# Pooled attention and token-mixing MLP: scores of four heads in one group on the array's row halves

## The chip, the cores and the metric

The kernel runs on one core of a Trainium2 chip. The metric is device time in microseconds of one execution; the profile is of one execution of the same program. The engines run side by side, each with its own queue in order: TensorE (PE in the profile, with PEld for its weight loads), VectorE (DVE), ScalarE (ACT), GpSimd (POOL) and SyncE (SP), whose queue issues most of the transfers.

## The reference

Attention over pooled keys and values, for 8 batches of 8 heads, 576 tokens and 64 channels a head, and then a ResMLP layer over its output:

```python
k_p = k.reshape(B, H, Sp, pool, D).mean(axis=3)          # pool = 8, Sp = 72
v_p = v.reshape(B, H, Sp, pool, D).mean(axis=3)
attn = softmax(scale * np.matmul(q, k_p.transpose(0, 1, 3, 2)))
x = np.matmul(attn, v_p)                                  # heads side by side: (B, 576, 512)

a1 = alpha1 * x + beta1
u = x + lam * np.einsum('ts,bsd->btd', w_tok, a1)         # mixing over tokens
a2 = alpha2 * u + beta2
out = u + lam * (np.maximum(a2 @ w_ch1, 0.0) @ w_ch2)     # 512 -> 2048 -> 512
```

## The kernel before, in words

**Two pipelines side by side.** The MLP runs in nine blocks of 512 tokens. In a block, `mlp_A(n, j)` (16 steps, four products each, L555) makes 128 of the 2048 hidden channels and ScalarE applies bias and relu from PSUM (L560, tile Hj); `mlp_B(n, m, part)` (16 steps of four products, L573) then accumulates the output of 128 tokens at a time, and VectorE adds it to u (L578). While the MLP works on block n, the attention of batch n+1 is fed in between its steps. Batch 0 stands ahead of the blocks; the last two blocks have no attention beside them.

**The order is written by hand.** Every piece of work has a slot number, and `sorted` over these numbers gives the order in which instructions are put into the engines' queues. Step j of `mlp_A` has the slot j, and the steps of `mlp_B` have the slots 16 to 31. Each engine works its own queue in that order, so a slot says what stands ahead of what, not when it happens.

**The attention of a batch**, for batches 2 to 7:

- `att_F`, `att_Frem`: q transposed by DMA into qT (four heads a tile) and rem_qT (the last 64 tokens of all heads). In qT a head has its even and its odd tokens' channels on the two halves of the partitions; in rem_qT the halves are the even and the odd heads.
- `att_K(b, u)`: pooled and transposed keys of four heads, both halves of the partitions holding the same keys. VectorE copies each half into a tile kpT whose other half holds zeros (L416).
- `att_S(b, h)`: scores of one head. Against the zero-padded keys a product over all 128 partitions picks out one half: one product of 256 columns for each half (L450), one of 64 columns for the last 64 tokens (L453); ScalarE takes the exponential of each half into ET (L455).
- `att_V`: pooled values on VectorE.
- `att_AV(b, h)`: five small products (L470, L474) that also give the sum of the weights in a column of their own; VectorE takes the reciprocal (L476) and multiplies (L478).
- `att_X`: for two heads at a time x times lam and alpha1, on VectorE, into xs (L485 and the small half L489).
- `mix_T(b, c)`: the mixing over tokens, five products of 512 columns (L518) that read xs of all eight heads, for four chunks of 128 tokens; the last 64 tokens of two batches share a chunk. VectorE adds x (L522) and scales (L525), and `mix_uT` transposes the result for the MLP.

In the first batch of this loop (b=1) transposes of q are done on TensorE, the pooled keys are copied by ScalarE, and the constants of the mixing are still being set up.

**PSUM.** Two pools hold the eight banks: six tiles named gp, which serve scores, K, attention products, mixing and `mlp_A`, and two named ch, which `mlp_B` accumulates in. Tiles of a pool are handed round in order of request, and a request waits until the earlier holder of the same tile has been read.

The functions that the diff touches are these:

Of the kernel before, what the change touches and what calls it, by code (L numbers as in the profile page):

```python
# [7 lines left out]
FP = mybir.dt.float32  # L8
F16 = mybir.dt.float16
BF = mybir.dt.bfloat16  # L10
AF = mybir.ActivationFunctionType
# [3 lines left out]
P = 128  # L15
SPG = 72
DM = 512
# [6 lines left out]
def kernel(  # L24
# [18 lines left out]
    nc = tc.nc  # L43
    ctx.enter_context(tc.manual_schedule())
    B, H, S, D = q.shape

    const = ctx.enter_context(tc.tile_pool(name="const", bufs=1))
    work = ctx.enter_context(tc.tile_pool(name="work", bufs=1))
    psA = ctx.enter_context(tc.tile_pool(name="psA", bufs=6, space=bass.MemoryType.PSUM))
    psB = ctx.enter_context(tc.tile_pool(name="psB", bufs=2, space=bass.MemoryType.PSUM))  # L50

    def gp(name):
        return psA.tile([P, 512], FP, tag="gp", name=name)
# [11 lines left out]
    st1 = {}  # L65
# [164 lines left out]
    load_v16(0)  # L230
    load_wtok()

    vp1_pool, kpT_pool, ET_pool = [], [], []
    for i in range(4):
        t = const.tile([SPG, 2, 66], F16, tag=f"vp1_{i}", name=f"vp1_{i}")
        nc.vector.memset(t, 8.0)
# [1 line left out]
        if i < 2:  # L238
            t = const.tile([P, 2, 4, SPG], BF, tag=f"kpT_{i}", name=f"kpT_{i}")
            nc.vector.memset(t, 0.0)  # L240
            kpT_pool.append(t)
    for i in range(H):
        t = const.tile([SPG, S + 64], F16, tag=f"ET_{i}", name=f"ET_{i}")
        nc.vector.memset(t[:, S:], 1.0)
        ET_pool.append(t)
    xs_pool = [const.tile([P, 5, DM], BF, tag=f"xs_{i}", name=f"xs_{i}") for i in range(2)]
    nc.vector.memset(xs_pool[1][0:64, 4, :], 0.0)
# [143 lines left out]
    def att_K(b, u, copy):  # L391

        st = st1[b]
        ps_kp = gp("ps_kp")
        kp = ps_kp[:, 0:4 * SPG].rearrange("p (h g) -> p h g", g=SPG)
        n, nr = (1, 1) if b else (4, 2)
        if not b:
            nc.vector.tensor_copy(out=st["k"][u][:, :, 4], in_=st["k"][u][:, :, 0])
            if u == 0:
                cast_rem_k(nc.vector)  # L400
        for h in range(4):
            for c in range(n):
                nc.tensor.matmul(  # L403
                    out=kp[:, h, 0:64],
                    lhsT=st["k"][u][:, h, c:c + 2].rearrange("p a d -> p (a d)"),
                    rhs=pool_main, start=(c == 0), stop=(c == n - 1))
        for hh in range(2):
            for c in range(nr):
                nc.tensor.matmul(  # L409
                    out=kp[:, hh:4:2, 64:72],  # L410
                    lhsT=st["rem"][1][:, hh, c:c + 2].rearrange("p a d -> p (a d)"),
                    rhs=pool_rem.rearrange("p (g u r) -> p u r g", r=2, u=2)[:, u],
                    start=(c == 0), stop=(c == nr - 1))
        for a in range(2):
            rows = slice(64 * a, 64 * a + 64)
            (copy or (nc.scalar.copy, nc.vector.tensor_copy)[a])(  # L416
                out=kpT_pool[u][rows, a], in_=kp[rows])
# [16 lines left out]
    def att_V(b, hp):  # L434

        t = st1[b]["v"][hp // 2][:, 2 * (hp % 2):2 * (hp % 2) + 2]
        for n in (4, 2):
            nc.vector.tensor_tensor(out=t[:, :, 0:n], in0=t[:, :, 0:n], in1=t[:, :, n:2 * n],  # L438
                                    op=ALU.add)
        nc.vector.tensor_tensor(out=vp1_pool[hp][:, :, 0:64], in0=t[:, :, 0], in1=t[:, :, 1],  # L440
                                op=ALU.add)

    def att_S(b, h):
        st = st1[b]
        u, r, hh = h // 4, h // 2 % 2, h % 2
        ET = ET_pool[h]
        for half in range(2):
            n0, n = 256 * half, 256 + 64 * half
            ps_sc = gp("ps_sc")
            nc.tensor.matmul(out=ps_sc[0:SPG, 0:256], lhsT=kpT_pool[u][:, half, h % 4, :],  # L450
                             rhs=st["qT"][u][:, 2 * (h % 4):2 * (h % 4) + 2, :])
            if half:
                nc.tensor.matmul(out=ps_sc[0:SPG, 256:320], lhsT=kpT_pool[u][:, hh, h % 4, :],  # L453
                                 rhs=st["rem_qT"][:, :, h // 2::4].rearrange("p c i -> p i c"))
            nc.scalar.activation(out=ET[:, n0:n0 + n], in_=ps_sc[0:SPG, 0:n],  # L455
                                 func=AF.Exp, bias=0.0, scale=0.125)
        st["ET"][h] = ET

    def att_AV(b, h):
        st = st1[b]  # L460
        if "x" not in st:
            st["x"] = st1[b - 1]["x"] if b % 2 else work.tile([P, 6, DM], FP, tag="x_tm", bufs=1, name="x_tm")
        hp, hh = h // 2, h % 2
        ET, vp1, x = st["ET"][h], vp1_pool[hp], st["x"]
        ps_av = gp("ps_av")
        av = ps_av[:, 0:5 * 66].rearrange("p (c x) -> p c x", x=66)
        odd = b % 2
        for c in range(4):
            m0 = 256 * (c % 2) + 128 * (c // 2)
            nc.tensor.matmul(out=av[:, odd + c, :], lhsT=ET[:, m0:m0 + 128],  # L470
                             rhs=vp1[:, hh, :])

        r0 = 512 - 64 * odd
        nc.tensor.matmul(out=av[:, 4 - 4 * odd, :], lhsT=ET[:, r0:r0 + 128], rhs=vp1[:, hh, :])  # L474
        rec = work.tile([P, 5], FP, tag="rec", bufs=2, name="rec")
        nc.vector.reciprocal(out=rec, in_=av[:, :, 64:65])  # L476
        dd = D * h
        nc.vector.tensor_tensor(out=x[:, 1 - odd:6 - odd, dd:dd + D], in0=av[:, :, 0:64],  # L478
                                in1=rec.unsqueeze(2).to_broadcast((P, 5, D)), op=ALU.mult)

    def att_X(b, h0, h1, eng=nc.vector):

        x, xs = st1[b]["x"], xs_pool[b % 2]
        cols = slice(D * h0, D * h1)
        eng.tensor_tensor(  # L485
            out=xs[:, 0:4, cols], in0=x[:, 1:5, cols],
            in1=lamal_bc[:, cols].unsqueeze(1).to_broadcast((P, 4, D * (h1 - h0))), op=ALU.mult)
        p0 = 64 * (b % 2)
        eng.tensor_tensor(out=xs[p0:p0 + 64, 4, cols], in0=x[p0:p0 + 64, 5 - 5 * (b % 2), cols],  # L489
                          in1=lamal_bc[p0:p0 + 64, cols], op=ALU.mult)  # L490
# [177 lines left out]
    def attention(b):  # L668


        first = b == 1
        todo = []
        if first:
            for hp in range(4):
                todo.append((2.6 + 0.9 * hp, lambda hp=hp: att_F(b, hp)))
            todo.append((3.5, lambda: cast_rem(b, nc.gpsimd)))
            todo.append((3.65, lambda: load_w2(3)))
            todo.append((7.4, lambda: att_Frem(b, nc.scalar.copy)))
        if b == 2:
            todo.append((-2.0, lambda: cast_rem(b, nc.gpsimd)))  # L680
            todo.append((-1.1, lambda: att_F(b, 0)))
            todo.append((-1.1, lambda: att_F(b, 2)))
            todo.append((0.2, lambda: att_Frem(b)))
        if 1 < b < B - 1:
            at = 14.0 if b == 2 else 10.0
            todo.append((at, lambda: att_F(b + 1, 0)))
            todo.append((at + 0.1, lambda: att_F(b + 1, 2)))
            todo.append((27.4, lambda: cast_rem(b + 1, nc.gpsimd)))
            todo.append((27.5, lambda: att_Frem(b + 1)))
        for u in range(2):  # L690
            todo.append((3.6 + 0.1 * u if first else -0.9 + 1.2 * u,
                         lambda u=u: sum_k(b, u, nc.gpsimd)))
            todo.append((6.4 + 3.0 * u if first else 4.1 + 2.0 * u,
                         lambda u=u: att_K(b, u, nc.scalar.copy if first else nc.vector.tensor_copy)))
            if first:
                todo.append((11.0 + 1.2 * u, lambda u=u: first_V(b, u, nc.scalar.copy)))
        for h in range(8):
            at = 8.8 + 1.1 * h if first else 7.4 + 1.15 * h
            lag = 3.3 if first else 2.0
            todo.append((at, lambda h=h: att_S(b, h)))  # L700
            todo.append((at + lag, lambda h=h: att_AV(b, h)))
            if h % 2:
                eng = nc.gpsimd if first and h < 7 else nc.vector
                todo.append((at + lag + 0.1, lambda h=h, eng=eng: att_X(b, h - 1, h + 1, eng)))
            elif not first:
                todo.append((0.2 + 1.0 * h, lambda h=h: att_V(b, h // 2)))
        for c in range(5):
            at = 21.8 + 1.2 * c if first else 19.1 + 1.3 * c
            if c < 4 or b % 2:
                todo.append((at, lambda c=c: mix_T(b, c)))  # L710
                key = (b, c) if c < 4 else (b - 1, 4)
                if first and c in (2, 3):
                    at += 1.3 * c - 2.0
                elif first and c < 2:
                    at += 1.0
                todo.append((at + 1.8, lambda key=key: mix_uT(key)))
        return todo

    for n in range(NBLK):
        todo = []  # L720
# [14 lines left out]
        b = n + 1  # L735
# [46 lines left out]
```

The softmax here doesn't subtract the row's maximum and nothing guards it: scores larger than these inputs give would overflow.

## Time and profile before

| what | before |
|---|---|
| median of 3 runs | 361.68 us (361.34 to 361.83) |
| span of the profiled execution | 360.4 us |
| TensorE busy | 345.3 us, 96% |
| VectorE busy | 209.5 us, 58% |
| ScalarE busy | 154.1 us, 43% |
| GpSimd busy | 86.6 us, 24% |
| mlp_A and mlp_B products, L555 and L573 | 138.1 and 133.7 us busy, 592 and 576 products |
| score products, L450 and L453 | 25.4 and 15.6 us busy, 128 and 64 products |
| exponentials, L455 | 44.8 us busy, 128 of them |

A product's busy time holds the passage through the array, which overlaps with the next product, so the spacing of starts says more of the cost than the busy time. A line of the timeline has the start, the length from the first start to the last end, the engine, the source line, the operation with what it writes and reads, shape and count, and in brackets the idle time ahead of it with what ended it. A line of a group ends with the busy time, the mean of one instruction in ns, and the engine's idle time before the group.

### The profile page before, as it was taken

What the parts mean: (1) busy time and instruction counts of PE and PEld (TensorE: products, weight loads), DVE (VectorE), ACT (ScalarE), POOL (GpSimd) and SP (SyncE); (2) the same over time, 40 slices, a digit from 0 to 9 for tenths busy, and PEclk for the clock granted to TensorE, in tenths of its full rate; (3) what the DMA queues carried; (4) which work ended last, traced back from release to release, by engine and by line L of the source; (5) the groups of instructions that cost most, each with busy time, mean ns of one, the idle gap of its engine ahead of it and who ended that gap; (6) DMA issues with size and microseconds to landing.
All of it is one profiled execution on the core that took longest, in us unless ns stands there. A gap on an engine that the chain in (4) does not pass through costs nothing.

```text
span 360.4 us, 5916 instructions
## 1 busy us (share of the span) xinstructions
PE 345.3 (96%) x2229; PEld 186.7 (52%) x2229; DVE 209.5 (58%) x452; ACT 154.1 (43%) x319; POOL 86.6 (24%) x99
## 2 busy tenths in 40 slices
PE   4988999899999999999999999999999999999994
PEld 1566765445644564456445644564456445545541
DVE  6484347688773778576748787677567870011011
ACT  2572995027900890069006900592059204704700
POOL 8469407261117000620052006200510000000000
PEclk9999999999999999999999999999999999999999
DMA  8999920977949872987199729872910132011012
GB/s 122 200 215 261 216 43 3 185 189 203 162 118 225 155 125 64 244 159 126 53 206 190 130 62 215 175 131 60 224 58 0 40 78 75 0 58 60 1 58 58
DMA packets 65886, 44.58 MB, mean 124 GB/s; under 512 B 32377, under 2 KB 57021, under 8 KB 65858
## 3 DMA queue, kind: packets, MB, share of 16 engines
q1 hardware_dynamic: 50480, 33.30, 38.6%
q0 software_dynamic: 15072, 10.76, 20.9%
q8 instruction: 17, 0.28, 0.3%
q10 hardware_dynamic: 306, 0.14, 0.2%
q14 instruction: 11, 0.09, 0.1%
HBM read 38.30 MB, written 9.44 MB: 132 GB/s over the span
## 4 chain that ended last, share of the span: by engine, by line
PE 89%; DVE 4%; ACT 3%; DMA 2%; SPq 1%; issue 1%; ACTq 0%; DVEq 0%
PE ps_ch L573 33%; PE ps_h L555 32%; PE ps_tok L518 11%; PE ps_sc L450 4%; PE ps_av L470 2%; DVE x_tm L478 2%; PE ps_sc L453 1%; ACT Hj L560 1%; DMA vecs<-in_moe_alpha_dram 1%; PE ps_bc L278 1%; PE ps_kp L403 1%; DMA rem_qT<-rem_q 1%; SPq L363 1%; DVE w L339 1%; PE ps_q L368 1%
## 5 line engine op out<-in xcount | busy, mean ns | idle before, releaser
L560 ACT ACTIVATE Hj<-ps_h,bias_cols 128x512 bf16<-128x512 f32 x144 | 98.8, 690 | 150.8 <-PE ps_h L555 149.9
L555 PE MATMUL ps_h<-u_fm,w 128*128 128x512 bf16 (+1 forms) x592 | 138.1, 374 | 1.4 <-ACT u_fm L541 1.1
L573 PE MATMUL ps_ch<-w,Hj 128*128 128x512 bf16 x576 | 133.7, 379 | 0.0
L573 PEld LDWEIGHTS <-Hj 128*128 128x128 bf16 x576 | 54.7, 98 | 62.7 <-issue 1.6
L555 PEld LDWEIGHTS <-w 128*128 128x128 bf16 x592 | 63.3, 114 | 45.7 <-issue 2.6
L578 DVE TENSOR_TENSOR u_sb<-u_sb,ps_ch 128x512 f32<-128x512 f32 x36 | 24.5, 688 | 75.1 <-PE ps_ch L573 74.7
L518 PE MATMUL ps_tok<-xs,wtT 128*128 128x512 bf16 (+3 forms) x200 | 44.5, 380 | 1.8 <-DVE xs L485 1.8
L455 ACT ACTIVATE ET<-ps_sc 72x256 f16<-72x256 f32 (+1 forms) x128 | 44.8, 405 | 2.6 <-PE ps_sc L450 2.5
L522 DVE TENSOR_TENSOR u_sb<-x_tm,ps_tok 128x512 f32<-128x512 f32 (+1 forms) x40 | 27.5, 687 | 19.5 <-PE ps_tok L518 19.4
L478 DVE TENSOR_TENSOR x_tm<-ps_av,rec 128x320 f32<-128x320 f32 x64 | 31.5, 492 | 2.5
L147 POOL CAST rem_q<-rem_raw 128x256 bf16<-128x256 f32 x7 | 2.9, 421 | 123.0 <-DMA rem_raw<-in_q_dram 123.0
L518 PEld LDWEIGHTS <-wtT 128*128 128x128 bf16 (+3 forms) x200 | 17.3, 100 | 23.6 <-issue 1.8
L438 DVE TENSOR_TENSOR v_u<-v_u 72x512 f32<-72x512 f32 (+1 forms) x48 | 27.5, 573 | 1.2
L525 DVE TENSOR_TENSOR u_bf<-u_sb,al_bc 128x512 bf16<-128x512 f32 x34 | 26.3, 775 | 1.2
L450 PE MATMUL ps_sc<-qT,kpT 128*72 128x256 bf16 x128 | 25.4, 278 | 0.1
L476 DVE RECIPROCAL rec<-ps_av 128x5 f32<-128x5 f32 x64 | 12.3, 192 | 21.1 <-PE ps_av L474 20.2
L470 PEld LDWEIGHTS <-ET 72*128 72x128 f16 x256 | 16.0, 97 | 11.9 <-issue 0.5
L162 POOL TENSOR_TENSOR k_raw<-k_raw 128x512 f32<-128x512 f32 x14 | 18.2, 1303 | 14.1 <-DMA k_raw<-in_k_dram 13.6
L164 POOL TENSOR_TENSOR k_bf<-k_raw 128x512 bf16<-128x512 f32 x14 | 19.0, 1354 | 1.1
L485 DVE TENSOR_TENSOR xs<-x_tm,lamal_bc 128x512 bf16<-128x512 f32 x26 | 18.3, 704 | 0.9
L470 PE MATMUL ps_av<-vp,ET 72*128 72x66 f16 x256 | 18.0, 193 | 0.3 <-ACT wtT L299 0.3
L416 DVE CAST kpT<-ps_kp 64x288 bf16<-64x288 f32 x26 | 11.8, 455 | 10.5 <-PE ps_kp L409 5.2
(111 smaller groups left out, 217.5 us busy)
## 6 DMA issues: line engine op xcount, KB each, us to landing
out_dram<-u_sb SPq DMA_DIRECT2D x32, 256.0 KB
k_raw<-in_k_dram SPq DMA_DIRECT2D x14, 512.0 KB
v_u<-in_v_dram SPq DMA_DIRECT2D x12, 512.0 KB
q_bf<-in_q_dram POOLq DMA_DIRECT2D x16, 256.0 KB, 7.0
w<-in_moe_w_ch_dram POOLq DMA_DIRECT2D x8, 512.0 KB, 11.3
v<-in_v_dram POOLq DMA_DIRECT2D x4, 256.0 KB, 7.5
out_dram<-u_sb SPq DMA_DIRECT2D x8, 128.0 KB
rem_raw<-in_q_dram SPq DMA_DIRECT2D x15, 64.0 KB
```

The costliest lines, as they stand in the source:

```text
L438: nc.vector.tensor_tensor(out=t[:, :, 0:n], in0=t[:, :, 0:n], in1=t[:, :, n:2 * n], op=ALU.add)
L450: nc.tensor.matmul(out=ps_sc[0:SPG, 0:256], lhsT=kpT_pool[u][:, half, h % 4, :], rhs=st["qT"][u][:, 2 * (h % 4):2 * (h % 4) + 2, :])
L455: nc.scalar.activation(out=ET[:, n0:n0 + n], in_=ps_sc[0:SPG, 0:n], func=AF.Exp, bias=0.0, scale=0.125)
L470: nc.tensor.matmul(out=av[:, odd + c, :], lhsT=ET[:, m0:m0 + 128], rhs=vp1[:, hh, :])
L478: nc.vector.tensor_tensor(out=x[:, 1 - odd:6 - odd, dd:dd + D], in0=av[:, :, 0:64], in1=rec.unsqueeze(2).to_broadcast((P, 5, D)), op=ALU.mult)
L518: nc.tensor.matmul(out=ps_tok[p0:p1], lhsT=wtT[0:kk, at, P * c:P * c + p1 - p0], rhs=xs_pool[i][0:kk, sc, :], start=(sc == 0), stop=(sc == 4))
L522: nc.vector.tensor_tensor(out=s["u"][p0:p1, :], in0=x[p0:p1, 1 + c if c < 4 else 5 - 5 * i, :], in1=ps_tok[p0:p1, 0:DM], op=ALU.add)
L525: eng.tensor_tensor(out=s["u_bf"], in0=s["u"], in1=al2_bc, op=ALU.mult)
L555: nc.tensor.matmul(out=ps_h[:, t0:t1], lhsT=w1_of(cc, j), rhs=u_fm[n][:, cc, t0:t1], start=(cc == 0), stop=(cc == 3))
L560: nc.scalar.activation(out=t, in_=ps_h, func=AF.Relu, bias=bias_cols[:, j:j + 1], scale=1.0)
L573: nc.tensor.matmul(out=ps, lhsT=Hj[n, j][:, 128 * m:128 * m + 128], rhs=w2[j // 4][:, j % 4, :], start=(j == 0), stop=(j == NJ - 1))
L578: nc.vector.tensor_tensor(out=u, in0=u, in1=ps, op=ALU.add)
```

## The change

For batches 1 to 7 the scores of four heads become one group, `att_S4(b, u)`. The keys are no longer padded with zeros: `att_K` copies them once into kp, and each product contracts over 64 partitions, on one half of the array's rows, so that the products of the even and of the odd tokens can work side by side. The two halves write to tiles of their own: four tiles of the pool gp and both of the pool ch, which `mlp_B` doesn't use in these slots. The exponentials then take 512 columns at a time (two heads of one half), and two more take the last 64 tokens of two heads each. The order of heads within a group becomes 2, 3, 0, 1; the attention products are given slots after the exponentials, and the mixing starts half a slot later. Batch 0 keeps its scores as they were.

```diff
+            kp_pool.append(const.tile([P, 4, SPG], BF, tag=f"kp_{i}", name=f"kp_{i}"))
-    for i in range(H):
-        t = const.tile([SPG, S + 64], F16, tag=f"ET_{i}", name=f"ET_{i}")
-        nc.vector.memset(t[:, S:], 1.0)
+    for i in range(2):
+        t = const.tile([SPG, 4, S + 64], F16, tag=f"ET_{i}", name=f"ET_{i}")
+        nc.vector.memset(t[:, :, S:], 1.0)
...
+        if b:
+            copy(out=kp_pool[u], in_=kp)
+            return
...
+    def att_S4(b, u):
+
+        st = st1[b]
+        qT, kp, rest = st["qT"][u], kp_pool[u], st["rem_qT"]
+        lo = [psB.tile([P, DM], FP, tag="ch", bufs=2, name="ps_s") for _ in range(2)]
+        hi = [gp("ps_s") for _ in range(2)]
+        r = [gp("ps_r")[0:SPG, 0:128].rearrange("p (h i) -> p h i", i=64) for _ in range(2)]
+
+        for i in range(4):
+            a = i % 2
+            nc.tensor.matmul(
+                out=r[a][:, i // 2], lhsT=kp[64 * a:64 * a + 64, i, :],
+                rhs=rest[64 * a:64 * a + 64, :, 2 * u + i // 2::4].rearrange("p c i -> p i c"))
+
+        for i in (2, 3, 0, 1):
+            for a in range(2):
+                rows = slice(64 * a, 64 * a + 64)
+                nc.tensor.matmul(
+                    out=(hi if i > 1 else lo)[a][0:SPG, 256 * (i % 2):256 * (i % 2) + 256],
+                    lhsT=kp[rows, i, :], rhs=qT[rows, 2 * i:2 * i + 2, :])
...
+        def exp(k):
+            if k < 2:
+                o, i = ET[:, k::2, 512:S], r[k]
+            else:
+                a, pair = k % 2, (hi, lo)[k // 2 - 1]
+                h = 2 if k < 4 else 0
+                o = ET[:, h:h + 2, 256 * a:256 * a + 256]
+                i = pair[a][0:SPG, :].rearrange("p (h i) -> p h i", i=256)
+            nc.scalar.activation(out=o, in_=i, func=AF.Exp, bias=0.0, scale=0.125)
...
-        for h in range(8):
-            at = 8.8 + 1.1 * h if first else 7.4 + 1.15 * h
-            lag = 3.3 if first else 2.0
-            todo.append((at, lambda h=h: att_S(b, h)))
-            todo.append((at + lag, lambda h=h: att_AV(b, h)))
-            if h % 2:
-                eng = nc.gpsimd if first and h < 7 else nc.vector
-                todo.append((at + lag + 0.1, lambda h=h, eng=eng: att_X(b, h - 1, h + 1, eng)))
-            elif not first:
-                todo.append((0.2 + 1.0 * h, lambda h=h: att_V(b, h // 2)))
+        for u in range(2):
+            at = (9.0 if first else 6.3, 12.3)[u]
+            todo.append((at, lambda u=u: att_S4(b, u)))
+            for k, dt in enumerate((0.1, 0.1, 0.1, 0.8, 1.8, 2.8)):
+                todo.append((at + dt, lambda u=u, k=k: st1[b]["exp", u](k)))
+            lag = 1.0 if first else 0.0
+            for i, dt in ((2, 2.7), (3, 3.2), (0, 5.0), (1, 5.5)):
+                h = 4 * u + i
+                todo.append((at + lag + dt, lambda h=h: att_AV(b, h)))
+                if i % 2:
+                    eng = nc.gpsimd if first and (u, i) != (1, 1) else nc.vector
+                    todo.append((at + lag + dt + 0.1,
+                                 lambda h=h, eng=eng: att_X(b, h - 1, h + 1, eng)))
+        if not first:
+            for hp in range(4):
+                todo.append((0.2 + 2.0 * hp, lambda hp=hp: att_V(b, hp)))
         for c in range(5):
-            at = 21.8 + 1.2 * c if first else 19.1 + 1.3 * c
+            at = 21.8 + 1.2 * c if first else 19.6 + 1.3 * c
```

For a batch from 2 on these numbers sort to the following order of the work on TensorE (S4, AV and X as above, A and B the MLP's steps, E the exponentials 0 to 5 of a group on ScalarE):

```
before: K1 A7 S0 A8 S1 A9 AV0 S2 A10 AV1 S3 A11 AV2 A12 S4 AV3 A13 S5 A14 AV4 S6 A15 AV5 S7
        B00 AV6 B01 AV7 B02 B03 mix0 B10 mix1 B11 mix2 B12 B13 mix3
after:  K1 S4(0) E012 A7 E3 A8 E4 A9 AV2 E5 AV3 A10 A11 AV0 AV1 A12 S4(1) E012 A13 E3 A14 E4 A15
        AV6 E5 AV7 B00 B01 AV4 AV5 B02 B03 mix0 B10 mix1 B11 B12 mix2 B13 mix3
```

More of the change, by code (lines that the diff above doesn't have):

```diff
@@ L231 @@
     load_wtok()
-    vp1_pool, kpT_pool, ET_pool = [], [], []
+    vp1_pool, kpT_pool, kp_pool, ET_pool = [], [], [], []
     for i in range(4):
@@ L445, in att_S @@
         u, r, hh = h // 4, h // 2 % 2, h % 2
-        ET = ET_pool[h]
+        ET = ET_pool[u][:, h % 4]
         for half in range(2):
@@ L457, in att_S @@
         st["ET"][h] = ET
+    def att_S4(b, u):
[15 more added lines that the diff above has]
+                    lhsT=kp[rows, i, :], rhs=qT[rows, 2 * i:2 * i + 2, :])
+        ET = ET_pool[u]
+        for i in range(4):
+            st["ET"][4 * u + i] = ET[:, i]
+        def exp(k):
[7 more added lines that the diff above has]
+            nc.scalar.activation(out=o, in_=i, func=AF.Exp, bias=0.0, scale=0.125)
+        st["exp", u] = exp
     def att_AV(b, h):
```

## The prediction

> **What bounds the kernel now.** I read the page's busy shares first, then the chain that ended last, then the timeline of one block. The page gives TensorE 96% of the span, and the chain puts nearly all of it on three matmul lines:
>
> ```profile
> PE 345.3 (96%) x2229; PEld 186.7 (52%) x2229; DVE 209.5 (58%) x452; ACT 154.1 (43%) x319; POOL 86.6 (24%) x99
> ...
> PE 89%; DVE 4%; ACT 3%; DMA 2%; SPq 1%; issue 1%; ACTq 0%; DVEq 0%
> ```
>
> A busy share proves nothing alone, since matmul ends are modelled. So I took the spacing of starts in the TensorE timeline of the block with b=5 (start, length, what):
>
> ```profile
> 196.69 0.38 PE L450 MATMUL ps_sc<-qT,kpT 128*72 128x256 bf16 x2
> 196.90 0.24 PE L453 MATMUL ps_sc<-rem_qT,kpT 128*72 128x64 bf16 x1
> 196.98 1.03 PE L555 MATMUL ps_h<-u_fm,w 128*128 128x512 bf16 x4
> 197.85 0.38 PE L450 MATMUL ps_sc<-qT,kpT 128*72 128x256 bf16 x2
> ...
> 199.01 0.29 PE L470 MATMUL ps_av<-vp,ET 72*128 72x66 f16 x4
> 199.13 0.20 PE L474 MATMUL ps_av<-vp,ET 72*128 72x66 f16 x1
> 199.17 0.38 PE L450 MATMUL ps_sc<-qT,kpT 128*72 128x256 bf16 x2
> ```
>
> The scores of a head hold TensorE for 196.98-196.69 = 0.29 us (0.11 for each 256-column product, 0.075 for the 64-column one), a step of mlp_A for 0.865, an attention product for 0.16; by the same reading K costs 0.17 and a mixing 1.08. For a block with four mixings: 27.62 (two stretches of 64 large products, each 13.81 in the blocks without attention) + 8 x 0.295 + 8 x 0.157 + 2 x 0.17 + 4 x 1.08 = 35.9. The chain has that block from 226.87 to 262.84, 35.97. So from the third batch on TensorE waits for nothing at all: time taken off its queue comes off the end, and every new wait in its queue goes onto the end.
>
> The margin, though, is thin in one place. VectorE in the same block, at the last two heads:
>
> ```profile
> 207.58 0.69 DVE L485 TENSOR_TENSOR xs<-x_tm,lamal_bc 128x512 bf16<-128x512 f32 x1
> 208.28 0.29 DVE L489 TENSOR_TENSOR xs<-x_tm,lamal_bc 64x128 bf16<-64x128 f32 x1
> 208.60 0.20 DVE L476 RECIPROCAL rec<-ps_av 128x5 f32<-128x5 f32 x1
> 208.83 0.49 DVE L478 TENSOR_TENSOR x_tm<-ps_av,rec 128x320 f32<-128x320 f32 x1
> 209.24 0.18 DVE L476 RECIPROCAL rec<-ps_av 128x5 f32<-128x5 f32 x1
> 209.46 0.49 DVE L478 TENSOR_TENSOR x_tm<-ps_av,rec 128x320 f32<-128x320 f32 x1
> 209.99 0.69 DVE L485 TENSOR_TENSOR xs<-x_tm,lamal_bc 128x512 bf16<-128x512 f32 x1
> ```
>
> The last xs ends at 210.68; the first mixing starts at 210.73, and the eight products ahead of it (from 208.96, 0.2155 each) had ended at 210.69. The mixing starts on the very moment its input is ready: no slack. From these lines: reciprocal to multiply 0.23, multiply to next reciprocal 0.41, multiply to xs 0.53, xs to its small half 0.70, that to the next reciprocal 0.32; and 0.355 from an attention product's start to its reciprocal (199.01 to 199.37).
>
> **What the Trainium skill says.** "TensorEngine Tiling (Array Packing)", Key Properties: row or column tiles work in parallel, and a change of tiling mode drains TensorE. The trace has no row halves, but it has column halves: the shared remainder chunk is mixed as ten products of 64 columns of weights in two halves.
>
> ```profile
> 219.14 0.38 PE L573 MATMUL ps_ch<-w,Hj 128*128 128x512 bf16 x1
> 219.45 1.27 PE L518 MATMUL ps_tok<-xs,wtT 128*64 128x512 bf16 x10
> 220.66 0.60 PE L573 MATMUL ps_ch<-w,Hj 128*128 128x512 bf16 x2
> ```
>
> Ten products take 220.66-219.14-0.2155 = 1.30 us where five full ones take 1.08: the halves do run together, and entering and leaving the mode costs 0.22. "TensorE: Matmul & The Clock Gate", Part 3, says that row groups overlap in the same way (four of them gave 3.07 times in its measurement), and its table of specifications that ScalarE and VectorE work in strict order. The timelines agree: a late item holds all behind it. "TensorEngine Tiling", Gotcha 1, asks for different PSUM banks for different row tiles; the change gives each half its own, and that is where its six PSUM tiles a group come from.
>
> **The change part by part.**
>
> *Scores.* Removed per group of four heads: 4 x 0.295 = 1.18 us. Added: two pairs of 64-column products and four pairs of 256-column ones. If halves pair up as the column halves do, 2 x 0.075 + 4 x 0.11 = 0.59, plus 0.22 for the mode: 0.81. Bounds: 0.59 without a drain; 8 x 0.11 + 4 x 0.075 + 0.22 = 1.40 if halves do not overlap. I take 0.81: 0.37 saved a group, 0.74 a batch (-0.44 to 1.18).
>
> *Exponentials.* From the rows by shape, a 256-column one lasts 0.376, a 320-column one 0.436: 0.94 ns a column, so 0.62 for 512 and 0.26 for 128. Two follow each other in 0.58 (197.53 to 198.11), 0.11 less each than they last; so I space 512 at 0.50 and 128 at 0.15. A group: 2 x 0.15 + 4 x 0.50 = 2.3, where 4 x 0.58 = 2.3 went before. The sum does not change; what changes is when a result is ready. A relu is spaced 0.58 and starts 0.26 after its products end.
>
> *Wait one: the second group for VectorE.* PSUM tiles of the pool of six are handed round in order. Counting from the first group's later heads: AV(0), AV(1), A12, hi, hi, r, r; so the second r takes AV(0)'s tile. From the start of AV(2), VectorE needs 0.355 + 0.23 + 0.41 + 0.23 + 0.53 + 0.70 + 0.32 = 2.77 before it takes AV(0), and its multiply ends at 2.77 + 0.23 + 0.49 = 3.49, released about 3.54. TensorE asks for the tile after 2 AV, A10, A11, 2 AV and A12, 0.31 + 1.73 + 0.31 + 0.865 = 3.21, plus 0.1 of mode change: it waits 0.23.
>
> *Wait two: mlp_B for the last exponentials.* The group borrows both accumulators of mlp_B. Set 0 at the start of the second group. With the 0.23, A13 starts at about 1.0 and A15 ends at 3.6. ScalarE, in order: relu A12 0.26, three exponentials to 1.65, relu A13 from 2.13 to 2.71, exp 3 to 3.21, relu A14 to 3.79, exp 4 to 4.41, with a release 4.5. TensorE reaches mlp_B's first product, which takes the accumulator of exp 4, at 3.6 + 0.31 = 3.9: it waits 0.58. Queued behind it is everything.
>
> *Wait three: mixing for xs.* AV(4) and AV(5) now come back to back, two mlp_B steps ahead of the first mixing (19.6 sorts into the place that 19.1 had; only the third mixing moves, behind one step). From AV(4)'s start TensorE reaches the mixing after 0.31 + 1.73 = 2.04; VectorE needs 0.355 + 0.23 + 0.41 + 0.23 + 0.53 + 0.70 = 2.45, and about 0.05 for the hand-over: it waits 0.45. Without wait two this one would be longer: VectorE, from AV(6) through AV(7), their xs, AV(4), AV(5) and xs, needs 4.9 where TensorE needs 4.07; the two waits together are never under 0.8.
>
> Waits one to three: 1.26 a batch, against 0.74 saved: +0.52, for six batches +3.1.
>
> *Batch 2.* Its rem_qT comes late. TensorE timeline of before:
>
> ```profile
> 85.87 1.03 PE L555 MATMUL ps_h<-u_fm,w 128*128 128x512 bf16 x4
> ...
> 86.74 0.38 PE L450 MATMUL ps_sc<-qT,kpT 128*72 128x256 bf16 x2
> ...
> 87.69 0.24 PE L453 MATMUL ps_sc<-rem_qT,kpT 128*72 128x64 bf16 x1 [0.57 <-DMA rem_qT<-rem_q]
> ```
>
> Before, A7 and two products stood ahead of the wait, and TensorE lost 87.69-86.96 = 0.73. The new group stands before A7 and begins with rem_qT: it is reached at 85.87 and starts at 87.69, 1.82 lost, 1.09 more.
>
> *Batch 1.* In that block ScalarE is busy 8.3 of 9 us and TensorE waits in several places (1.1 us at the first mixing). Scores save 0.74 and part goes into the wait on scale_w2 and xs that stands there anyway: I put it at -0.5.
>
> *Nothing.* The kp copy (one of 0.46 for two) and the earlier VectorE work lie in TensorE's shade; fewer memsets lie in the loads at the start; the transposes of u, a step later, feed a block that starts eight or more steps on.
>
> Sum: 3.1 + 1.1 - 0.5 = +3.7; 361.7 + 3.7 = 365.4.
>
> **The rivals.** (a) The waits do not show, and the row halves pay: 14 x 0.37 = 5.2 off, batch 2 gives back 1.1, batch 1 the 0.2 it fell short: 357.8. For it: TensorE is the bound everywhere. Against: the mixing has no slack now, and its two last heads come closer to it. (b) Halves overlap without any drain: 1.18 saved a batch against 1.26 of waits, +0.5 in six batches, +0.6 from the first two: 362.8; with one wait somewhat smaller, no change. For it: the drain is known only from column halves. (c) Halves do not overlap: 0.59 more a group than in the sum, 14 x 0.59 = 8.3, some of it inside waits: 372. Against: the ten column halves.
>
> **How the numbers follow.** My sum 0.58; (b), with all between 361 and 363.3, 0.17; (a) 0.15; (c) 0.10. Range 359.8 to 369.0: it holds the sum with a wait of half or double size and (b), and leaves out most of (a) and (c). Faster 0.19 ((a), and a quarter of (b)), same 0.08, slower 0.73.
>
> **What would show it.** Right: a group of scores holding TensorE for about 0.8; in each later block an idle gap before the first ps_ch released by ScalarE's ET, and one before the first ps_tok released by VectorE's xs; blocks of 36.5 rather than 35.97; in batch 2 a gap of 1.8 on rem_qT. Wrong: blocks under 35.9, gaps missing, or the score group under 0.6 or over 1.2.

## The result, and the profile after

| | before | after |
|---|---|---|
| median | 361.75 us (361.34 to 362.13, 4 runs) | 363.66 us (363.10 to 364.42, 4 runs) |
| ratio to before | | 1.0054 (95% interval 1.0031 to 1.0077) |
| span of the profiled execution | 360.4 us | 361.4 us |

The change made the kernel slower, by half a percent. Six more runs gave 363.33 us and a ratio of 1.0046 (1.0033 to 1.0059). The two spans lie closer together than the medians because the profiled execution of before was the slowest of its four (362.13 us) and that of after the fastest (363.10).

The page after, with the same two lines as were shown of before (busy times, and the shares of the chain that ended last):

```profile
PE 340.3 (94%) x2189; PEld 178.8 (49%) x2229; DVE 202.3 (56%) x434; ACT 149.8 (41%) x289; POOL 87.8 (24%) x99
...
PE 82%; DVE 7%; ACT 6%; DMA 2%; issue 1%; ACTq 0%; SPq 0%; DVEq 0%
```

TensorE is busy 5 us less, and the span is longer. Part of the 5 us is not work saved: this trace lacks 40 of the 2229 product records, and a second execution with all of them has 341.7 us, 3.6 less than before. In the chain TensorE fell from 89% to 82%, and VectorE and ScalarE together rose from 7% to 13%, with the same shares in the second execution: TensorE now waits. The TensorE timeline of the block with b=5 shows first what was gained. A group of four heads:

```profile
196.15 0.20 PE L410 MATMUL ps_kp<-pool_rem,rem_k 128*128 128x16 bf16 x2
196.28 0.35 PE L473 MATMUL ps_r<-rem_qT,kp 64*72 64x64 bf16 x4
196.46 0.61 PE L480 MATMUL ps_s<-qT,kp 64*72 64x256 bf16 x8
197.03 2.75 PE L595 MATMUL ps_h<-u_fm,w 128*128 128x512 bf16 x11
```

K's last product is through at about 196.20 (the last of its two starts in L410 and the usual 0.03 us), and mlp_A goes on at 197.03: 0.82 us for four heads, where four times 0.295 went before. And further down in the same timeline, what was lost:

```profile
206.40 0.28 PE L510 MATMUL ps_av<-vp,ET 72*128 72x66 f16 x4
206.52 0.19 PE L514 MATMUL ps_av<-vp,ET 72*128 72x66 f16 x1
206.55 0.29 PE L510 MATMUL ps_av<-vp,ET 72*128 72x66 f16 x4
206.68 0.19 PE L514 MATMUL ps_av<-vp,ET 72*128 72x66 f16 x1
207.15 1.89 PE L613 MATMUL ps_ch<-w,Hj 128*128 128x512 bf16 x8 [0.28 <-ACT ET L495]
...
209.18 1.89 PE L613 MATMUL ps_ch<-w,Hj 128*128 128x512 bf16 x8
211.36 1.24 PE L558 MATMUL ps_tok<-xs,wtT 128*128 128x512 bf16 x4 [0.28 <-DVE xs L525]
```

The last attention product (the one at 206.68) is through at 206.71, and mlp_B starts at 207.15: 0.44 us of waiting for an exponential. The bracket says 0.28 because it counts from the end of the product's passage through the array, not from where the next could have started. Eight products from 209.18 end at 210.91, and the mixing starts at 211.36: 0.45 us of waiting for xs. VectorE's timeline says why:

```profile
209.23 0.20 DVE L516 RECIPROCAL rec<-ps_av 128x5 f32<-128x5 f32 x1
209.46 0.49 DVE L518 TENSOR_TENSOR x_tm<-ps_av,rec 128x320 f32<-128x320 f32 x1
209.87 0.18 DVE L516 RECIPROCAL rec<-ps_av 128x5 f32<-128x5 f32 x1
210.09 0.49 DVE L518 TENSOR_TENSOR x_tm<-ps_av,rec 128x320 f32<-128x320 f32 x1
210.62 0.69 DVE L525 TENSOR_TENSOR xs<-x_tm,lamal_bc 128x512 bf16<-128x512 f32 x1
```

Two heads back to back, each waiting for the one before it on VectorE, end at 211.31; before, the second-last head had been finished a step of mlp_B earlier.

The lengths of the blocks (from the first mlp_A product of one to that of the next) put the account together. The last three columns are of runs described below:

| block with | before | after | after again | three edits | three edits, padded keys |
|---|---|---|---|---|---|
| ahead of the first block | 32.86 | 32.97 | 32.75 | 33.17 | 33.30 |
| b=1 | 46.62 | 46.17 | 46.16 | 46.06 | 46.68 |
| b=2 | 36.69 | 37.06 | 37.47 | 36.07 | 37.48 |
| b=3 (five mixings) | 37.29 | 37.53 | 37.52 | 36.49 | 37.23 |
| b=4 | 35.95 | 36.08 | 36.08 | 35.20 | 35.94 |
| b=5 (five mixings) | 37.29 | 37.53 | 37.53 | 36.49 | 37.23 |
| b=6 | 35.96 | 36.09 | 36.18 | 35.20 | 35.94 |
| b=7 (five mixings) | 37.29 | 37.53 | 37.52 | 36.49 | 37.23 |

The later batches lose 0.13 (even) and 0.24 us (odd) each, the third batch (b=2) 0.37 and 0.78, and the second (b=1) gains 0.45 and 0.46. What stands ahead of the first block differs by up to 0.55 us between these five executions, the two of the same kernel by 0.22, so a difference of that size in the first row says nothing.

The third batch waits for rem_qT. The timeline of after there:

```profile
84.15 1.19 SPq L382 DMA_TRANSPOSE rem_qT<-rem_q  x1
...
85.48 0.20 PE L410 MATMUL ps_kp<-pool_rem,rem_k 128*128 128x16 bf16 x2
...
86.58 0.35 PE L473 MATMUL ps_r<-rem_qT,kp 64*72 64x64 bf16 x4 [0.90 <-DMA rem_qT<-rem_q]
...
87.30 0.41 PE L595 MATMUL ps_h<-u_fm,w 128*128 128x512 bf16 x1
```

From K's end at 85.53 to mlp_A at 87.30 are 1.77 us where a group takes 0.82: 0.95 lost. In the second execution it is 1.37, from 85.30 to 87.49.

### The profile page after: what moved, and what is told of

Its sections match the earlier page's. It is cut to its first block, busy times and chain, and to the rows that moved or that the text cites. A ratio compares the mean times of both kernels' runs of the same rounds, so it can differ in the third digit from the quotient of the medians.

```text
span 361.4 us, 5805 instructions
## 1 busy us (share of the span) xinstructions
PE 340.3 (94%) x2189; PEld 178.8 (49%) x2229; DVE 202.3 (56%) x434; ACT 149.8 (41%) x289; POOL 87.8 (24%) x99
## 3 DMA queue, kind: packets, MB, share of 16 engines
q1 hardware_dynamic: 50480, 33.30, 37.7%
## 4 chain that ended last, share of the span: by engine, by line
PE 82%; DVE 7%; ACT 6%; DMA 2%; issue 1%; ACTq 0%; SPq 0%; DVEq 0%
PE ps_ch L613 31%; PE ps_h L595 30%; PE ps_tok L558 11%; DVE x_tm L518 3%; ACT Hj L600 3%; ACT ET L495 2%; DVE xs L525 2%; PE ps_s L480 2%; PE ps_av L510 1%; DMA vecs<-in_moe_alpha_dram 1%; PE ps_bc L279 1%; PE ps_r L473 1%; DVE rec L516 1%; PE ps_kp L404 1%; PE ps_q L369 1%
## 5 line engine op out<-in xcount | busy, mean ns | idle before, releaser
L595 PE MATMUL ps_h<-u_fm,w 128*128 128x512 bf16 (+1 forms) x572 | 132.0, 374 | 2.6 <-ACT u_fm L581 1.1
L613 PE MATMUL ps_ch<-w,Hj 128*128 128x512 bf16 x564 | 131.7, 379 | 2.6 <-ACT ET L495 1.7
L595 PEld LDWEIGHTS <-w 128*128 128x128 bf16 x592 | 64.2, 114 | 53.5 <-issue 2.9
L495 ACT ACTIVATE ET<-ps_s 72x512 f16<-72x512 f32 x56 | 33.4, 596 | 0.0
L442 DVE TENSOR_TENSOR v_u<-v_u 72x512 f32<-72x512 f32 (+1 forms) x48 | 28.3, 589 | 0.8
L162 POOL TENSOR_TENSOR k_raw<-k_raw 128x512 f32<-128x512 f32 x14 | 19.1, 1365 | 9.2 <-DMA k_raw<-in_k_dram 5.8
L510 PEld LDWEIGHTS <-ET 72*128 72x128 f16 x256 | 13.1, 97 | 7.1 <-issue 0.7
L510 PE MATMUL ps_av<-vp,ET 72*128 72x66 f16 x256 | 14.4, 193 | 0.3 <-ACT wtT L300 0.3
L79 POOL DMA_DIRECT2D q_bf<-in_q_dram x16 | 12.4, 776 | 7.5 <-DVE q_bf L78 5.6
L581 ACT COPY u_fm<-ps_uT 128x512 bf16<-128x512 bf16 x8 | 4.6, 587 | 22.9 <-PE ps_uT L579 22.9
```

The costliest lines, as they stand in the source:

```text
L495: nc.scalar.activation(out=o, in_=i, func=AF.Exp, bias=0.0, scale=0.125)
L595: nc.tensor.matmul(out=ps_h[:, t0:t1], lhsT=w1_of(cc, j), rhs=u_fm[n][:, cc, t0:t1], start=(cc == 0), stop=(cc == 3))
L613: nc.tensor.matmul(out=ps, lhsT=Hj[n, j][:, 128 * m:128 * m + 128], rhs=w2[j // 4][:, j % 4, :], start=(j == 0), stop=(j == NJ - 1))
```

## The experiments

All kernels compute the whole result. Their times are compared with runs of before on the same chip (361.75 to 361.88 us).

**The changed kernel again.**

> The changed kernel once more, unaltered, in more rounds, to settle how much slower it is: the median so far stands 1.9 us above before, the two profiled executions only 1.0 us apart. If the six later batches cost what their profiled blocks show (0.13 or 0.24 us each, 0.4 in the third batch), 362.7; if the executions vary by what the third batch waits for rem_qT, up to 364.4.

Measured 363.33 us (6 runs), ratio 1.0046 (1.0033 to 1.0059). Between the two figures. The execution profiled here loses 0.78 us in the third batch where the first had lost 0.37, so that batch does vary: TensorE came to the group 0.23 us earlier, and the transpose of rem_qT was issued 0.19 us later (84.34).

**Zero-padded keys in the new order.**

```diff
-        if b:
-            copy(out=kp_pool[u], in_=kp)
-            return
...
-                out=r[a][:, i // 2], lhsT=kp[64 * a:64 * a + 64, i, :],
+                out=r[a][:, i // 2], lhsT=kp[:, a, i, :],
...
-                    lhsT=kp[rows, i, :], rhs=qT[rows, 2 * i:2 * i + 2, :])
+                    lhsT=kp[:, a, i, :], rhs=qT[:, 2 * i:2 * i + 2, :])
```

(kp is here the padded kpT.)

> Groups, exponentials, slots and waits as in the changed kernel, but every score product over all 128 rows against zero-padded keys, as before. My theory: the halves do run side by side and save 1.18 - 0.82 = 0.36 us a group, so without them the fourteen groups cost up to 14 x 0.36 = 5.0 us more than the changed kernel, a little less where a wait takes it up: 366.5 to 368.7. Rival (the halves save nothing, mode changes eat it): no different from the changed kernel, 363.7.

Measured 368.11 us, ratio 1.0175 (1.0159 to 1.0191): 4.8 us above the changed kernel, against 5.0 worked out (VectorE's second copy of the keys is back too). Its TensorE timeline has the group over all rows:

```profile
199.50 0.49 PE L470 MATMUL ps_r<-rem_qT,kpT 128*72 128x64 bf16 x4
199.82 1.04 PE L477 MATMUL ps_s<-qT,kpT 128*72 128x256 bf16 x8
200.70 2.54 PE L592 MATMUL ps_h<-u_fm,w 128*128 128x512 bf16 x11
```

1.20 us from 199.50 to 200.70, where the halves take 0.82. The row halves are worth what they were meant for; with padded keys, the rest of the change stands 6.3 us above before.

**The mixing a step later.**

```diff
-            at = 21.8 + 1.2 * c if first else 19.6 + 1.3 * c
+            at = 21.8 + 1.2 * c if first else 20.6 + 1.3 * c
```

> The mixing one slot later (20.6 in place of 19.6), so that one more step of mlp_B stands ahead of it. My theory: the first mixing waits 0.45 us for xs in each of the six later batches, and nothing else; the wait goes, 6 x 0.45 = 2.7 us less than the changed kernel: 361.0. Rival (TensorE only waits elsewhere instead, because VectorE or the next block's inputs are the bound): no change, 363.7.

Measured 360.80 us, ratio 0.9966 (0.9953 to 0.9979): 2.5 us less than the changed kernel, and under before. Its blocks are shorter by 0.44 or 0.45 each. The wait for xs is real, and nothing takes its place.

**The exponentials a step earlier.**

```diff
-            for k, dt in enumerate((0.1, 0.1, 0.1, 0.8, 1.8, 2.8)):
+            for k, dt in enumerate((0.1, 0.1, 0.1, 0.1, 0.8, 1.8)):
```

> The exponentials of a group one step of mlp_A earlier: the fourth right behind the third, the fifth and sixth a slot earlier. My theory: ScalarE stands idle before relu A13 and mlp_B's first product waits 0.45 us for the fifth exponential; that wait goes, but VectorE then comes to the mixing no earlier and 0.3 to 0.4 of it comes back as a longer wait for xs, so 0.3 to 1.0 us less than the changed kernel over six batches: 362.7 to 363.4. Rival (the two waits are independent): 2.7 us less, 361.0.

Measured 362.11 us (21 runs), ratio 1.0013 (1.0006 to 1.0021): 1.2 us less than the changed kernel, above the range of my theory and less than half of the rival's. The blocks are shorter by 0.08 (odd) and 0.29 (even), some 0.8 us in five. The chain of waits of this kernel, b=5:

```profile
206.91 0.21 DVE rec L516
...
208.29 0.69 DVE xs L525
208.98 0.01 issue
209.00 0.29 DVE xs L529
209.28 0.03 issue
209.32 0.21 DVE rec L516
...
210.70 0.70 DVE xs L525
211.40 0.04 issue
211.44 1.24 PE ps_tok L558 x5
```

From the first reciprocal of head 6 to the mixing VectorE is never free for more than 0.04 us, in the lines left out too: the two waits lie one behind the other, and taking the first away uncovers the second. By the spacing of starts the wait for xs grows from 0.45 to 0.82 us in odd batches and to 0.59 in even ones, while the wait for the exponential (0.44) is gone.

**Both edits.**

> The mixing one slot later and the exponentials one step earlier together. My theory: with the wait for the exponential gone VectorE's chain is what the mixing waits for, and with the extra step ahead of the mixing that wait goes too: 0.9 us less in each of six batches than the changed kernel's 363.4, so 358.0, under before. Rival (the gains of the two edits simply add, 2.5 and 1.2): 359.6.

Measured 357.93 us, ratio 0.9899 (0.9885 to 0.9914). The theory's figure to 0.1 us: the two edits together are worth 5.4, more than the sum of what each gave alone.

**xs of two heads behind the next two heads.**

```diff
-                    todo.append((at + lag + dt + 0.1,
+                    late = 2.4 if b > 1 and (u, i) == (0, 3) else 0.1
+                    todo.append((at + lag + dt + late,
```

> Wait one alone: in the first group of a batch the xs of heads 2 and 3 is put behind the reciprocal and multiply of heads 0 and 1 on VectorE, so that the PSUM tile of head 0 is free when the second group asks for it. My theory: the second group holds TensorE for 0.82 and not 0.97, 6 x 0.15 = 0.9 us less than the changed kernel: 362.5. Rival (the second group is longer for other reasons, such as its weights): no change, 363.4.

Measured 363.10 us, ratio 1.0034 (1.0020 to 1.0047): only 0.2 less where 0.9 was expected, an interval that holds the changed kernel's ratio too, so the times alone don't show a gain; the trace does. The second group of b=5 in the TensorE timeline, first of the changed kernel, then of this one:

```profile
202.91 0.34 PE L473 MATMUL ps_r<-rem_qT,kp 64*72 64x64 bf16 x4
203.09 0.69 PE L480 MATMUL ps_s<-qT,kp 64*72 64x256 bf16 x8
203.78 0.84 PE L595 MATMUL ps_h<-u_fm,w 128*128 128x512 bf16 x2
```

```profile
203.22 0.35 PE L473 MATMUL ps_r<-rem_qT,kp 64*72 64x64 bf16 x4
203.40 0.60 PE L480 MATMUL ps_s<-qT,kp 64*72 64x256 bf16 x8
203.94 0.41 PE L595 MATMUL ps_h<-u_fm,w 128*128 128x512 bf16 x1
```

0.87 from the group's first product to mlp_A became 0.72, so the wait was there and goes. The odd blocks are 0.15 shorter (37.38), but those of b=4 and b=6 are as long as they were: only three batches had it. In even batches of the changed kernel the small half of xs starts before the large one has ended, and the next reciprocal comes 0.80 us after the large one's start (165.27 to 166.07, b=4) where it takes 1.03 in odd ones (201.35 to 202.38, b=5).

**All three edits of order.**

> All three edits: mixing later, exponentials earlier, xs behind. My theory: 0.9 below the previous kernel with two of them, 357.1; blocks of four mixings at 35.95 - 0.72 = 35.2. Rival (a new wait comes up as TensorE is faster, on a relu's PSUM tile or on VectorE): 358 or more.

Measured 357.48 us, ratio 0.9881 (0.9865 to 0.9896). That is 0.45 below the two edits, not 0.9, and the intervals overlap. The blocks show why: the even ones, 35.20 as worked out, were that long with two edits already, and the odd ones went from 36.64 to 36.49. The chain of waits of b=5, from the last three steps of mlp_A to the mixing:

```profile
200.88 2.71 PE ps_h L595 x12
...
203.90 1.73 PE ps_ch L613 x8
...
205.93 2.59 PE ps_ch L613 x12
208.52 1.08 PE ps_tok L558 x5
```

No other engine is in it any more; the lines left out are attention products.

**And the third batch's first group a step later.**

```diff
-            at = (9.0 if first else 6.3, 12.3)[u]
+            at = (9.0 if first else 7.3 if b == 2 else 6.3, 12.3)[u]
```

> As the previous one, and in the third batch (b=2) the first group a slot later, behind A7, as the scores of before stood. My theory: that group waits 1.2 us for rem_qT and one step of mlp_A takes 0.86 of it up: 356.3. Rival (the step moved only shifts the wait to the second group, which now comes right behind): 357.1.

Measured 357.07 us, ratio 0.9870 (0.9855 to 0.9886), the lowest of all; but its interval overlaps with the previous kernel's, and its third batch takes 36.00 against 36.07. The group still starts 2.44 us after the transpose of rem_qT was issued (84.06 to 86.51; 2.43 in the previous kernel), so the wait for it is halved, from 0.87 to 0.43 us, and the mlp_A step behind the group waits another 0.37 for VectorE's copy of keys. That accounts for the 0.07. My theory failed; the rival's time came out, but the wait is not at the second group, where it had put it. Whether the edit gains anything is open.

**The three edits without the halves.**

> The three edits of order (mixing later, exponentials earlier, xs behind) with zero-padded keys, so without the row halves. My theory: the order alone earns nothing, since before had no wait to remove; TensorE has the work of before and no more waits: 14 x 0.36 = 5.0 above the 357.5 of the three edits with halves, so 361.5 to 362.5, the time of before. Rival (the new order is worth something by itself, through longer exponentials or fewer instructions): under 361.

Measured 363.15 us, ratio 1.0032 (1.0019 to 1.0045): 1.1 above the range's middle, outside it. Its later blocks are those of before to 0.06 us (35.94 and 37.23), so there the order earns nothing by itself, as I said. What I had left out is the third batch: it takes 37.48, 0.79 more than before, because the group that begins with rem_qT loses 1.54 us there where before lost 0.73. Another 0.44 of this execution lies ahead of the first block; whether that is more than the spread between executions is open.

**The row halves entered twice a group.**

```diff
-        for i in (2, 3, 0, 1):
...
+        pairs((2, 3))
+        st["lo", u] = lambda: pairs((0, 1))
...
+            todo.append((at + 0.75, lambda u=u: st1[b]["lo", u]()))
```

> The three edits with halves, and each group cut in two: the products of its heads 0 and 1 come after the next full-array work instead of before it, so that TensorE enters and leaves the row halves twice a group. My theory: entering and leaving costs 0.22 a time, 14 x 0.22 = 3.1 above 357.5: 360.6, and any wait that the later results cause on top. Rival (the 0.82 of a group is the products themselves and the mode costs next to nothing): 357.5.

Measured 361.83 us, ratio 0.9997 (0.9988 to 1.0005): 4.35 above the three edits. The split-off pairs in its TensorE timeline:

```profile
197.49 0.41 PE L481 MATMUL ps_s<-qT,kp 64*72 64x256 bf16 x4
197.83 0.41 PE L599 MATMUL ps_h<-u_fm,w 128*128 128x512 bf16 x1
```

The mlp_A step ahead is through at 197.40; mlp_A goes on at 197.83, after 0.43, of which two pairs need 0.22. So 0.21 for entering and leaving, 2.9 in fourteen groups; the other 1.4 is about the 1.3 us that the trace lists, in six waits, for mlp_A behind a relu. Which wait would come had not been foreseen.

**Before with its mixing a step later.**

> The kernel before, with only its mixing one slot later. My theory: before has no slack at the mixing but no wait either, so nothing is gained: 361.8, at most 0.2 lower. Rival (before waits there as well, and a later mixing would have helped it as it helped the changed kernel): 360 or less.

Measured 361.77 us, ratio 0.9998 (0.9990 to 1.0006): no gain. Before had no wait at that place, though it had no slack either.

## Why the prediction was right, and where its sizes were off

The direction and the mechanism hold: the row halves save what was worked out, and waits that the new order makes eat more than that. The size was 3.7 us; measured are 1.9 and, in more runs, 1.5. The sign was less safe than it looks: 0.13 to 0.24 us a batch is what is left of two sums near 1.

- **A group of scores: 0.81.** Measured 0.82. The bound from the column halves carried over; "TensorEngine Tiling (Array Packing)", Key Properties, says that a change of mode drains TensorE, and the run with two entries puts 0.21 us on it. Padded keys cost 4.8 us more, so the halves' side-by-side work is shown by removal. No run puts both halves into one PSUM bank, so whether each half needed tiles of its own is not shown.
- **Wait one: 0.23 in each batch.** Mis-sized: 0.15, and in the three odd batches only. I had taken VectorE's spacings from an odd batch. Also, the tile that is waited for is the second one of the large products, not of the small ones.
- **Wait two: 0.58.** Measured 0.44. Relus and exponentials follow a little closer than I allowed (0.48 after an exponential, not 0.50), the last one takes 0.59, not 0.62, and it hands over 0.05 after its end.
- **Wait three: 0.45.** Measured 0.45, and removed by one step. That the waits lie one behind the other is what the earlier exponentials showed; "never under 0.8" held in odd batches (0.82) and not in even ones (0.59).
- **Six batches: +0.52 each, 3.1.** Measured +0.24 in odd and +0.13 in even ones from the fourth batch on. The waits sum to 1.05 and 0.88, not 1.26.
- **Third batch: 1.1 more on rem_qT.** The largest term that failed. TensorE loses 0.95 and 1.37 us there, not 1.82, so 0.22 and 0.64 more than the 0.73 of before. With the 0.13 of an even batch that is the whole of 0.37 and 0.78; the prediction had 1.6. rem_qT came early: its transpose was issued at 84.15 and 84.34 and not at 85.36. I had carried the old time over as if nothing ahead of it could move.
- **Second batch: -0.5.** Measured -0.45 and -0.46 in its block. How much of the 0.74 saved would be lost in waits was a guess; which wait took it, the runs don't say.

Of the rivals, (a) no waits and (c) no overlap are refuted by the traces. So is (b), no drain, by the 0.21 us a change of mode costs, though its 362.8 lies nearer to the measured 363.3 and 363.7 than my 365.4: by luck, since the drain it left out made up for waits that it had as long as I did. The likeliest was right with its waits a third too long.

## What to carry to other kernels

Where the bound engine has no waits, a shorter stage on it is only worth what the engines behind it can follow: work out each chain that a following stage waits for, with the spacing of starts, before and after regrouping. Grouping saves mode changes but delivers results in lumps; a fixed order of work has to be moved with it, here by one step each for the mixing and the exponentials, which turned 1.5 us slower into 3.8 us faster. When two waits lie one behind the other, removing the earlier alone shows little (1.2 us here) while removing the later shows its own share (2.5); together they gave 5.4, so try them together.

## What the runs showed of the hardware that was not expected

In both traces of the old order (before, and before with its mixing later) a VectorE operation ahead of the second block, u_bf, is stretched. The timeline of before:

```profile
76.45 1.26 POOL L162 TENSOR_TENSOR k_raw<-k_raw 128x512 f32<-128x512 f32 x1 [0.56 <-DVE u_sb L522]
76.46 1.80 DVE L525 TENSOR_TENSOR u_bf<-u_sb,al_bc 128x512 bf16<-128x512 f32 x1
...
79.01 0.37 SPq L580 DMA_DIRECT2D out_dram<-u_sb  x1
```

And in that of after:

```profile
76.12 0.69 DVE L565 TENSOR_TENSOR u_bf<-u_sb,al_bc 128x512 bf16<-128x512 f32 x1
...
77.56 0.37 SPq L620 DMA_DIRECT2D out_dram<-u_sb  x1
...
78.39 1.27 POOL L162 TENSOR_TENSOR k_raw<-k_raw 128x512 f32<-128x512 f32 x1 [0.16 <-DMA k_raw<-in_k_dram]
```

Beside a GpSimd sum that had started 10 ns earlier the same operation takes 1.80 us (1.58 in the other trace of the old order) and not 0.69. The Trainium skill, "SBUF — State Buffer", in "SBUF: two separate sides", says that a VectorE instruction with two SBUF inputs and a GpSimd one that reads SBUF share a pair of ports which the one that starts first holds for its whole instruction. The traces agree: in both, u_bf ends 0.55 us after the sum does (77.71 to 78.26 here), though it had started 0.01 us after the sum in one and 0.23 in the other, and a VectorE sum that reads PSUM beside the same kind of GpSimd sum takes its usual 0.69 (78.48 in after, beside the GpSimd sum at 78.39).

The first store behind u_bf was issued 1.45 us later in before (79.01 against 77.56), and the transpose of rem_qT on the same queue 1.2 us later. That the stretch made all of the second difference is not shown: with the three edits and padded keys u_bf takes 0.69, and the transpose was issued at 85.48 all the same, in a block that began 0.5 us later than before's. In the new order the sum starts after 77.8 and misses u_bf.
